# Lending the idle two-bank tile to the scans in an attention and Fourier-mixing kernel

## The chip, the cores and the metric

The kernel runs on one core of one Trainium2 chip. The metric is the device time of one execution in microseconds. Three runs of the kernel before gave a median of 1719.29 us (1718.14 to 1720.03).

Six names stand for the parts of a core. TensorE (PE in the profile) multiplies matrices and writes into PSUM, a small memory of eight banks; a bank holds 512 float32 values for each of 128 partitions. Its weight loads have a row of their own (PEld). VectorE (DVE) and ScalarE (ACT) work element by element and can read PSUM. GpSimd (POOL) works on SBUF alone. SyncE (SP) issues transfers. Each engine takes its instructions strictly in the order in which the program lists them, and waits on semaphores where one needs another's result or a buffer that another still uses.

## What is computed

The input `x` is 2048 tokens of 512 numbers. Two mixings of it are weighed by a gate per token:

```
g = sigmoid(sum(x * gate_w))
a = softmax attention of x, 32 heads of 16, 2048 x 2048 scores each, then @ wo
b = real part of the Fourier transform along the 512 and along the 2048
    a' = x @ dft_hid_re.T ; b' = x @ dft_hid_im.T
    y  = dft_seq_re @ a' - dft_seq_im @ b'
out = g * a + (1 - g) * b
```

The weights `wqkv` and `wo` are scaled up by 64, so the scores are large and the softmax needs the maximum of every row of scores before it can take exponentials.

## The kernel before

The kernel works in two stages. The front (to about 649 us) computes queries, keys and values, then the Fourier part's first product along the 512, then the larger part of its second product along the 2048. The second stage runs attention proper, with the rest of the Fourier part and the output projection between its steps.

To keep float32 accuracy every operand of a product is split into a high and a low part, and each product is three matmuls. `halves_of` (line 199) issues each of these as two matmuls, on the upper and the lower 64 rows of the array, which run side by side and write two PSUM banks; the two banks are added later. Here "product pair" means such two matmuls. They are all recorded under line 203.

**Scans.** The row maxima are found ahead of the attention. A scan covers 128 queries and 512 keys for the two heads of a pair; there are 64 for each of 16 pairs. 740 of them run in the front, woven between the product pairs. A scan in the front (`scan_folded`, line 159) has two halves, j = 0 and j = 1, one per head. A half is one matmul into one bank (line 172). Then, for every even block of keys, ScalarE copies the bank with a ReLU into an SBUF tile `fold` (line 176); for every odd block VectorE adds the bank to `fold` and takes the maximum along the row (line 178). The keys had been prepared as differences, so that sum and ReLU together give the maximum of both blocks.

**Slots and pace.** `products` and the loop of the spectral part call `beside` after each product pair. That is a slot. `beside` counts it, runs what `after` has put off to this slot, and issues a scan whenever the pace says so: one in 2.03 slots (`PART`) through most of the spectral part, one in 2.85 (`SWAP`) where operands are exchanged. When scan n comes, its half j = 0 is issued, and right behind it the half j = 1 of scan n - 1 (`behind`), so that the two matmuls fall on different rows of the array and run side by side.

**PSUM.** Four banks are two wide tiles of two banks, `wide0` and `wide1`; the products of one output tile accumulate in one of them and the next output tile takes the other (`xy`). The other four banks are the beds of the scans, `d0`, `d1`, `k0`, `k1`: an even block of keys goes to d, an odd one to k, the number is j. So a half of a scan finds its bank free when the same half two scans before has been read.

**The spectral part.** From about 326 us on, an output tile t is 48 slots: 16 steps of three product pairs. Its coefficients are loaded on SyncE's queue and split by GpSimd. At the end of a tile ScalarE reads its first bank at once (`tx`) and the second five slots later (`ty`), both scaled by `gm`; GpSimd adds them. The other wide tile meanwhile takes the next t. So for most of the 48 slots one wide tile holds no data that is needed. Tiles 14 and 15, and later 0 and 1 of the second half (`ph` = 1), are computed two at a time and use both wide tiles.

**What sets the order.** The order on each engine is written out by the program: the loops, `after` and the pace. A framework adds the semaphore waits. It takes them from tiles: whoever writes into a tile waits for those who have read it, and a new tile in the place of an old one (same tag) waits for the uses of the old. The pools here release whole tiles (`reuse_waits="tile"`).

Of the kernel before, what the change touches and what calls it, by code (L numbers as in the profile page):

```python
# [24 lines left out]
NB = S // P  # L25
# [40 lines left out]
def build(tc, xT, wqkv, wo, wrT, wiT, cr, ci, ct, gate, out):  # L66
    nc = tc.nc
    with ExitStack() as ctx:
# [90 lines left out]
        def scan_folded(n, j, bank, pool):  # L159

            p, i = SEQ[n]
            qb, c = i // 4, i % 4
            if i == 0 and j == 0:
                new_maxima(p)
                if p in PARTS:
                    nc.vector.memset(mx[p], -3.0e38)
            qs, ks = scanned[p]  # L170
            b, ps = 64 * j, bank(f"{'dk'[c % 2]}{j}")
            nc.tensor.matmul(ps, qs[b:b + 48, qb * P:(qb + 1) * P], ks[b:b + 48, c * 512:(c + 1) * 512],  # L172
                             start=True, stop=True)
            if c % 2 == 0:
                fold[j] = pool.tile([P, 512], F32, tag=f"fold{j}", name="fold")
                nc.scalar.activation(fold[j], ps, AF.Relu)  # L176
            else:
                nc.vector.tensor_tensor_reduce(out=fold[j], in0=ps, in1=fold[j], scale=1.0, scalar=-3.0e38,  # L178
                                               op0=ALU.add, op1=ALU.max, accum_out=mx[p][:, j, qb, c // 2:c // 2 + 1])
# [28 lines left out]
        turns = [0]  # L208

        def wide(i, name):  # L210
            return psf.tile([P, 2, 512], F32, tag=f"wide{i}", name=name)
# [21 lines left out]
        def narrow(tag, name):  # L233
            return psk[0].tile([P, 512], F32, tag=tag, name=name)

        def bank():

            order_.append(order_.pop(0))
            return narrow(order_[-1], "s2")
# [27 lines left out]
        seen, slots, due, count = [0], [0], [], [0]  # L267
        pace = [None, 0.0]
        with ExitStack() as pf:
# [3 lines left out]

            pss1 = []

            def xy():
                turns[0] += 1
                ps = wide(turns[0] % 2, "xy")
                return ps[:, 0, :], ps[:, 1, :]

            def after(n, f, *args):

                count[0] += 1
                due.append((slots[0] + n, count[0], f, args))
# [3 lines left out]
            def run_due(force=(False, False)):  # L288

                while True:  # L290
                    ready = [d for d in due if d[0] <= slots[0] or force[d[2] in maxima]]
                    if not ready:
                        return
                    d = min(ready, key=lambda d: d[:2])
                    due.remove(d)
                    d[2](*d[3])  # L296
# [88 lines left out]
            def begin_folds():  # L385

                banks.close()
                psk.append(ctx.enter_context(tc.tile_pool(name="psk", bufs=1, space=PSUM, reuse_waits="tile")))
                beds.extend((lambda tag: narrow(tag, "s"), fp))

            with ExitStack() as px:
                wb = px.enter_context(tc.tile_pool(name="wb", bufs=1))
# [235 lines left out]
            with ExitStack() as py:  # L628
                cp = py.enter_context(tc.tile_pool(name="cp", bufs=2, reuse_waits="tile"))
                def fetch(n):  # L630
                    if n < len(coef):
                        load_coef(n, cp.tile([P, CS, P], F32, tag="craw", name="craw", bufs=7))

                for n in range(4, 10):
                    fetch(n)
                for d in range(4):
                    after(4 + 6 * d, split_operand, NB - 4 + d, tail[:, d, :], nc.gpsimd)
                scan_at(SWAP)
                after(24, scan_at, PART)
                pss, yre, early = {}, {}, {}  # L640

                def go_ahead(k):

                    if k == 0:
                        assert seen[0] == FRONT, (seen, pace)
                        scanned.update(unfolded)
                        sums.append(narrow("k1", "pvb"))
                        nc.vector.memset(sums[0], 0.0)
                    if k == 1:
                        e = next_eb()  # L650
                        ahead.append(qk_single(0, 0, 0, [e[:, j, :] for j in range(2)]))
                    elif k == 2:
                        scan(seen[0], wide(1 - SCANS_IN, "s1"))
                        seen[0] += 1
                    else:
                        ahead.append(qk_both(0, 0, k // 3))

                def mixed(ph, t, yre, tx, ty):
                    y = cp.tile([P, D], F32, tag="y", name="y")
                    nc.gpsimd.tensor_add(y, tx, ty)  # L660
                    if ph:
                        nc.gpsimd.tensor_add(y, y, yre)
                    after(14, nc.sync.dma_start, y_d[t // 4][:, t % 4, :], y)

                for n, (ph, t, u) in enumerate(coef):
                    prepare(n + 3)
                    fetch(n + 10)
                    if u == 0 and (ph, t) == (0, NB - 1):
                        scan_at(SWAP)
                    if u == 2 and (ph, t) == (1, 0):  # L670
                        scan_at(PART)
                    if n == len(coef) - 2 * NU:
                        for _ in load_use(0):
                            pass
                        unfolded[PART_PAIR], loads = row_loads(PART_PAIR, nc.sync)
                        for load in loads:
                            load()
                    hi, lo = ready.pop(n)
                    if u == 0:
                        pss[t] = xy()  # L680
                        if ph:
                            yre[t] = cp.tile([P, D], F32, tag="yre", name="yre")
                            nc.sync.dma_start(yre[t], y_d[t // 4][:, t % 4, :])
                    if (ph, t, u) == (0, NB - 3, 0):
                        for i in range(2):
                            raw = stk.tile([P, 4, D], F32, tag="stk", name="early")
                            for d in range(4):
                                early[4 * i + d] = raw[:, d, :]
                                after(24 * i + 6 * d, nc.sync.dma_start, raw[:, d, :], ab_d[1][4 * i + d])
                    swap = (ph, t) == (0, NB - 1)  # L690

                    def renew(s):
                        raw = early.pop(s)
                        ah[s], al[s] = block(2 * s), block(2 * s + 1)
                        nc.scalar.copy(ah[s], raw)
                        after(4, (nc.gpsimd if s % 4 == 3 else nc.vector).tensor_sub, al[s], raw, ah[s].bitcast(F32))
                        if s >= 8 and s + 5 < NB:
                            early[s + 5] = load_operand(1, s + 5, cp)

                    for w in range(CS):  # L700
                        s = u * CS + w
                        for i, (c_, a_) in enumerate(((hi, ah[s]), (hi, al[s]), (lo, ah[s]))):
                            halves_of(pss[t], c_[:, w, :], a_, s == 0 and i == 0, s == NB - 1 and i == 2)
                            beside()
                            if n >= len(coef) - NU and 3 * s + i in AHEAD:
                                go_ahead(AHEAD.index(3 * s + i))
                        if swap:
                            if 3 <= s < 8:
                                early[s + 5] = load_operand(1, s + 5, cp)
                            after(1 + 5 * (s % 8) + 4 * (s // 8), renew, s)  # L710
                    if u == NU - 1:
                        tx = cp.tile([P, D], F32, tag="tx", name="tx")
                        last = n == len(coef) - 1
                        ty = cp.tile([P, D], F32, tag="raw" if last else "ty", name="ty", bufs=5 if last else 2)
                        if last:
                            for v, ps in zip((tx, ty), pss[t]):
                                nc.vector.tensor_scalar_mul(v, ps, gm[:, t:t + 1])
                        else:
                            nc.scalar.mul(tx, pss[t][0], gm[:, t:t + 1])
                            after(5, nc.scalar.mul, ty, pss[t][1], gm[:, t:t + 1])  # L720
                        after(10, mixed, ph, t, yre.get(t), tx, ty)
                run_due((True, True))

        assert seen[0] == FRONT + 1 and turns[0] % 2 == SCANS_IN, (seen, turns)
# [580 lines left out]
```

## Time and profile before

| | |
|---|---|
| median of 3 runs | 1719.29 us |
| profiled execution, time | 1718.53 us |
| its span | 1716.7 us |
| TensorE busy | 1702.1 us |
| ScalarE busy | 1535.5 us |
| VectorE busy | 1158.0 us |
| GpSimd busy | 726.6 us |
| scans in the front: matmuls, 1480 | 58.8 to 649.0 us |
| granted TensorE clock | 0.999 |

How to read it: the span is the profiled execution from its first instruction to its last, and its time has 1.8 us around that. A row of a timeline gives start, duration, engine, line, operation, what is written and read, and how many instructions are merged; in brackets stands the idle time before and what ended it. A row of the table of waits reads "who waits, its line <- whom, its line: us in total, times, longest". A row of the table by stretches gives, for each engine, its busy time and in brackets its instructions. "Busy" of TensorE counts matmuls that overlap and whose ends are modelled, so a busy TensorE can still be waiting a little.

### The profile page before, as it was taken

The numbers are of one execution on the slowest core, as the hardware profiler recorded it, in microseconds if no ns is written. First come the engines' busy times: TensorE is split into PE (matmuls) and PEld (weight loads), VectorE is DVE, ScalarE is ACT, GpSimd is POOL, SyncE is SP. The second block draws the span as 40 slices with busy tenths as digits, with TensorE's granted clock in tenths as the row PEclk, the third lists the DMA queues.
The fourth block names the chain that finished last, engine by engine and source line by source line (L and its number), as shares of the span: only waits on it lengthen the run. The fifth ranks groups of instructions, "written<-read, shape, count | busy, mean of one in ns | idle before, by whom it ended". The sixth has DMA issues, their size and how long they took to land.

```text
span 1716.7 us, 36848 instructions
## 1 busy us (share of the span) xinstructions
PE 1702.1 (99%) x13560; PEld 1027.3 (60%) x13560; DVE 1158.0 (67%) x2310; ACT 1535.5 (89%) x2548; POOL 726.6 (42%) x875
## 2 busy tenths in 40 slices
PE   9999999999999999999999999999999999999998
PEld 6888888888989784333333333334555555555554
DVE  5788988899999996666666666666212456653343
ACT  5798889888888888999999999999888888888876
POOL 4352233855555761444455364444223333334222
PEclk9999999999999999999999999999999999999999
DMA  8783444634344774455445354453426465575833
GB/s 284 243 299 74 130 145 160 202 113 118 113 118 137 197 147 100 120 126 123 133 119 136 93 142 123 114 153 73 91 63 144 134 148 148 142 174 151 197 88 126
DMA packets 149573, 242.04 MB, mean 141 GB/s; under 512 B 50144, under 2 KB 60880, under 8 KB 142800
## 3 DMA queue, kind: packets, MB, share of 16 engines
q1 hardware_dynamic: 134128, 218.32, 46.6%
q0 software_dynamic: 14688, 20.33, 5.0%
q8 instruction: 106, 1.74, 0.5%
q10 hardware_dynamic: 576, 1.05, 0.2%
q14 instruction: 75, 0.61, 0.1%
HBM read 156.24 MB, written 83.11 MB: 139 GB/s over the span
## 4 chain that ended last, share of the span: by engine, by line
PE 94%; DMA 2%; DVE 1%; issue 1%; ACT 1%; POOL 1%; SPq 0%; DVEq 0%; POOLq 0%; ACTq 0%
PE pvb L751 28%; PE xy L203 23%; PE s L228 18%; PE s L172 11%; PE s L203 9%; PE s L153 4%; DVE fold L178 1%; DMA raws<-wqkv 0%; ACT fold L176 0%; DMA q_d<-eh 0%; DMA raws<-xT 0%; PE s L548 0%; DVE y L866 0%; POOL s L296 0%; DMA k_d<-eh 0%
## 5 line engine op out<-in xcount | busy, mean ns | idle before, releaser
L252 ACT ACTIVATE eb<-s 128x1024 f32<-128x1024 f32 x512 | 576.6, 1126 | 66.4 <-PE s L228 66.4
L260 ACT ACTIVATE e<-s 128x512 f32<-128x512 f32 x1022 | 606.9, 705 | 0.0
L178 DVE CUSTOM_DVE_ANT_0 fold<-s,fold 128x512 f32<-128x512 f32 x740 | 496.7, 690 | 53.7 <-PE s L172 17.2
L751 PE MATMUL pvb<-eb,va 128*17 128x512 f32 x2052 | 511.5, 597 | 0.0
L751 PE MATMUL pvb<-e,va 128*17 128x512 f32 x2044 | 510.7, 597 | 0.0
L176 ACT ACTIVATE fold<-s 128x512 f32<-128x512 f32 x740 | 435.2, 603 | 72.7 <-PE s L172 46.9
L155 DVE TENSOR_REDUCE mx<-s 128x2 f32<-128x1024 f32 x284 | 348.0, 1225 | 173.6 <-PE s L153 173.5
L228 PEld LDWEIGHTS s<-qs,ks 50*128 50x128 f32 x2048 | 214.7, 184 | 349.3 <-ACT eb L252 242.2
L228 PE MATMUL s<-qs,ks 50*128 50x512 f32 x2048 | 417.3, 434 | 0.0
L203 PE MATMUL xy<-b,c 64*128 64x512 f32 x2304 | 377.7, 392 | 1.2 <-DVE b L347 1.0
L172 PE MATMUL s<-ks,qs 48*128 48x512 f32 x1480 | 366.3, 406 | 2.1 <-DVE mx L178 0.7
L203 PEld LDWEIGHTS xy<-b,c 64*128 64x128 f32 x2304 | 264.4, 187 | 17.3 <-DVE b L347 1.4
L172 PEld LDWEIGHTS s<-ks,qs 48*128 48x128 f32 x1480 | 199.8, 184 | 57.7 <-DVE mx L178 17.8
L751 PEld LDWEIGHTS pvb<-eb,va 128*17 128x17 f32 x2052 | 71.3, 96 | 191.5 <-issue 183.0
L203 PE MATMUL s<-b,b 64*128 64x512 f32 x1050 | 136.8, 391 | 0.1
L770 POOL DMA_DIRECT2D r_d<-lc x31 | 18.0, 580 | 262.3 <-DVE lc L769 215.1
L203 PE MATMUL xy<-w,b 64*128 64x512 f32 x768 | 123.3, 392 | 0.0
L763 POOL DMA_DIRECT2D lc<-ob x124 | 63.0, 515 | 130.8 <-DVE ob L760 120.5
L153 PE MATMUL s<-ks,qs 48*128 48x512 f32 x568 | 114.7, 394 | 0.0
L203 PEld LDWEIGHTS s<-b,b 64*128 64x128 f32 x1050 | 100.3, 185 | 24.0 <-issue 1.0
L378 POOL TENSOR_TENSOR c<-craw,c 128x512 fp32r<-128x512 f32 x76 | 99.8, 1313 | 6.1
L772 POOL DMA_DIRECT2D rb<-r_d x124 | 60.4, 494 | 96.3 <-DMA r_d<-lc 91.3
(143 smaller groups left out, 1587.9 us busy)
## 6 DMA issues: line engine op xcount, KB each, us to landing
qs<-q_d SPq DMA_DIRECT2D x68, 256.0 KB
craw<-cr SPq DMA_DIRECT2D x60, 256.0 KB
craw<-ct SPq DMA_DIRECT2D x48, 256.0 KB
ks<-k_d SPq DMA_DIRECT2D x42, 256.0 KB
kept_None<-sum SPq DMA_DIRECT2D x40, 256.0 KB
craw<-kept_None SPq DMA_DIRECT2D x40, 256.0 KB
qs<-q_d SPq DMA_DIRECT2D x68, 128.0 KB
craw<-ci SPq DMA_DIRECT2D x32, 256.0 KB
```

The costliest lines, as they stand in the source:

```text
L153: nc.tensor.matmul(ps[:, j, :], qs[b:b + 48, qb * P:(qb + 1) * P], ks[b:b + 48, c * 512:(c + 1) * 512], start=True, stop=True)
L155: nc.vector.tensor_reduce(mx[p][:, :, qb, c], ps, axis=AX.X, op=ALU.max)
L172: nc.tensor.matmul(ps, qs[b:b + 48, qb * P:(qb + 1) * P], ks[b:b + 48, c * 512:(c + 1) * 512], start=True, stop=True)
L176: nc.scalar.activation(fold[j], ps, AF.Relu)
L178: nc.vector.tensor_tensor_reduce(out=fold[j], in0=ps, in1=fold[j], scale=1.0, scalar=-3.0e38, op0=ALU.add, op1=ALU.max, accum_out=mx[p][:, ...
L203: nc.tensor.matmul(ps[j], lhs[r], rhs[r], start=first, stop=last)
L228: nc.tensor.matmul(pss[j], ks[b:b + 50, kb * P:(kb + 1) * P], qs[b:b + 50, q0:q0 + 512], start=True, stop=True)
L252: nc.scalar.activation(e, ps, AF.Exp, scale=SCALE)
L260: nc.scalar.activation(e[j], pss[j], AF.Exp, scale=SCALE)
L378: sub(lo, raw, hi.bitcast(F32))
L751: nc.tensor.matmul(pvb[r:r + VC, :], va[:, kb, 2 * p + j, :], es[c][j], start=kb == 0, stop=kb == NB - 1, tile_position=(0, r))
L763: nc.gpsimd.dma_start(lc[32 * n:32 * n + 32, :], ob[r + DH:r + VC, :].rearrange("p (s e) -> p s e", e=16))
```

## The change

`bank(...)` of the scans is no longer chosen by the parity of the key block but by a function `bed`. The two wide tiles are allocated once, as `sides`, for the whole front, and `xy` hands out their banks by turns. At the end of an output tile t, with 0 < t < 13, `spare` notes which side that tile has used and a stretch of slots, from 12 to 44 after the current one. While the slot count lies in it, `bed` has three places for a scan: d, k and the spare side ("w"); it takes the one that was dealt longest ago. Outside it there are d and k. A scan keeps its place for both halves: bank j of the side, or the bed with number j. Pace, scans, readers and all other code stay.

```diff
@@ scan_folded
-            b, ps = 64 * j, bank(f"{'dk'[c % 2]}{j}")
+            b, ps = 64 * j, bank(n, j)
@@
+            sides = [wide(i, "xy") for i in range(2)]
+            spare = [0, 0, 0]
+            places, taken = {"d": -2, "k": -1}, {}
+
             def xy():
                 turns[0] += 1
-                ps = wide(turns[0] % 2, "xy")
+                ps = sides[turns[0] % 2]
                 return ps[:, 0, :], ps[:, 1, :]
+
+            def bed(n, j):
+
+                if j == 0:
+                    side, since, until = spare
+                    free = ["d", "k"] + ["w"] * (since <= slots[0] < until)
+                    at = min(free, key=lambda a: places.get(a, -3))
+                    places[at] = n
+                    taken[n] = at, side
+                at, side = taken[n]
+                return sides[side][:, j, :] if at == "w" else narrow(f"{at}{j}", "s")
@@ begin_folds
-                beds.extend((lambda tag: narrow(tag, "s"), fp))
+                beds.extend((bed, fp))
@@ the spectral part
-                pss, yre, early = {}, {}, {}
+                pss, yre, early, side_of = {}, {}, {}, {}
@@
                         pss[t] = xy()
+                        side_of[t] = turns[0] % 2
@@ at the end of tile t
                         after(10, mixed, ph, t, yre.get(t), tx, ty)
+                        if 0 < t < NB - 3:
+                            spare[:] = side_of[t], slots[0] + 12, slots[0] + 44
```

## The prediction

> **What bounds the kernel now.** I read the page first (engines, slices, chain), then the stretches of the spectral part one by one, then the order of single instructions there.
>
> ```profile
> span 1716.7 us, 36848 instructions
> PE 1702.1 (99%) x13560; PEld 1027.3 (60%) x13560; DVE 1158.0 (67%) x2310; ACT 1535.5 (89%) x2548; POOL 726.6 (42%) x875
> PE 94%; DMA 2%; DVE 1%; issue 1%; ACT 1%; POOL 1%; SPq 0%; DVEq 0%; POOLq 0%; ACTq 0%
> PE pvb L751 28%; PE xy L203 23%; PE s L228 18%; PE s L172 11%; PE s L203 9%; PE s L153 4%; DVE fold L178 1%; DMA raws<-wqkv 0%; ACT fold L176 0%; DMA q_d<-eh 0%; DMA raws<-xT 0%; PE s L548 0%; DVE y L866 0%; POOL s L296 0%; DMA k_d<-eh 0%
> ```
>
> TensorE ends nearly everything: 94% of the chain. So a microsecond that TensorE loses in its own queue is lost to the kernel, and a saving elsewhere counts only if TensorE was waiting for it. In the spectral part (about 326 to 649 us) the queue holds product pairs (L203) with scans (L172) between them.
>
> ```profile
> core 0: us, PE busy (x) PEld busy (x) DVE busy (x) ACT busy (x) POOL busy (x), PEclk, DMA share, GB/s
> 490.00:520.00 30.00, 30.00 (x256) 25.47 (x254) 28.46 (x85) 26.32 (x46) 15.96 (x17) 1.00 0.47 132
> 580.00:610.00 30.00, 29.67 (x243) 24.23 (x241) 28.36 (x75) 25.39 (x47) 21.61 (x19) 1.00 0.84 199
> ```
>
> An undisturbed stretch issues 256 matmuls in 30 us, 0.234 us per concurrent pair; the granted clock is 1.00. What waits there for a bank is this:
>
> ```profile
> engine line waited for: us in total, times, longest us
> PEld s L172 <- DVE mx L178: 8.7, 35, 0.7
> PEld s L172 <- ACT fold L176: 4.7, 16, 0.3
> PEld s L172 <- DVE mx L178: 0.5, 2, 0.3
> ```
>
> The first two rows are the whole spectral part, 326 to 650 us; the third is 407 to 418 us, the part of one tile in which the change lends its idle neighbour. Asked over all 14 such parts, seven show this row at all, with 0.2 to 0.5 each and 2.4 us together. So the waits that a third place for the scans can remove are about 2.4 us, 0.14% of the time. VectorE is 95% busy in the undisturbed row, but it does not hold TensorE up there.
>
> **The rhythm of the scans.** TensorE, ScalarE and VectorE over two and a half microseconds of that part:
>
> ```profile
> 485.46 0.45 PE L172 MATMUL s<-ks,qs 48*128 48x512 f32 x2
> 485.70 0.69 PE L203 MATMUL xy<-b,c 64*128 64x512 f32 x4
> 486.17 0.46 PE L172 MATMUL s<-ks,qs 48*128 48x512 f32 x2
> 486.40 0.69 PE L203 MATMUL xy<-b,c 64*128 64x512 f32 x4
> 486.87 0.46 PE L172 MATMUL s<-ks,qs 48*128 48x512 f32 x2
> ...
> 485.95 1.24 ACT L176 ACTIVATE fold<-s 128x512 f32<-128x512 f32 x2 [0.16 <-PE s L172]
> ...
> 486.01 0.69 DVE L178 CUSTOM_DVE_ANT_0 fold<-s,fold 128x512 f32<-128x512 f32 x1
> ...
> L172 PE MATMUL s<-ks,qs x1480: 386/397/502, 58.8 to 649.0; 48*128 48x512 f32 x185
> ```
>
> Each L172 row of two is the first half of one scan and, 0.06 to 0.07 us later (0.46 less one matmul of 0.397), the second half of the scan before. The rows are 0.70 us apart, so a second half starts 0.77 us after its own first half. The reading of a first half ends later than that: the first half at 485.46 is read by VectorE at 486.01 for 0.69, to 486.70, 1.24 us after it started; the one at 486.17 is read by the second of the two ScalarE instructions, which end at 487.19, 1.02 us after.
>
> **The change, part by part.**
>
> *Order of work.* Instruction for instruction, all five engines and the DMA queues keep their order: 740 scans at the same pace, the same 1480 matmuls, 740 reads. Only banks, and so waits, change. Nothing is moved past anything, so cost 0: there is no instruction or transfer that would need new cover.
>
> *One tile object per side instead of a new one per product.* Within `products` nothing changes; ten waits of TensorE on its own earlier matmuls go. Cost 0: the matmul waited for is long done in TensorE's own queue; were each a release of 0.07 us (below), it would be 0.7 us gained.
>
> *The lent place.* From 12 to 44 slots after a product ends, `bed` deals three places in turn, so every third scan goes to the wide tile: 78 scans in 14 stretches, 38 read by ScalarE and 40 by VectorE. Its two halves are two banks of one tile object. Beds `d` and `k` are two tiles of one bank each. The program as built draws the consequence: in all 78 lent scans the matmul of the second half carries a wait for the instruction that reads the first half, although that lies in the other bank. In the kernel before, a second half waits only for the reading of the scan two before it. So the wait comes 0.77 us after the first half starts, and what it waits for ends at 1.02 or 1.24. Behind it on TensorE's queue stands everything: the product pairs and the next scan; nothing passes it.
>
> The trace has one clean wait of this kind, of another cause, which prices the restart:
>
> ```profile
> 415.27 0.44 PE L172 MATMUL s<-ks,qs 48*128 48x512 f32 x2
> 415.97 0.78 PE L172 MATMUL s<-ks,qs 48*128 48x512 f32 x2
> 416.87 0.59 PE L172 MATMUL s<-ks,qs 48*128 48x512 f32 x2
> 417.67 0.48 PE L172 MATMUL s<-ks,qs 48*128 48x512 f32 x2
> ...
> 416.26 0.18 PEld L172 LDWEIGHTS s<-ks,qs 48*128 48x128 f32 x1 [0.33 <-DVE mx L178]
> ...
> 415.50 0.69 DVE L178 CUSTOM_DVE_ANT_0 fold<-s,fold 128x512 f32<-128x512 f32 x1 [0.39 <-PE xy L203]
> ```
>
> VectorE ends at 416.19 and the weight load goes at 416.26: 0.07 from release to start. The second matmul of the row at 415.97 was due at about 416.02 and so came 0.24 late. The next two rows stand 1.70 us after it instead of 1.40, so 0.24 of waiting cost 0.30: restarting, with its weights not loaded ahead, takes 0.06 more. By the third row the pair is 0.48 wide again, so each third scan meets the old rhythm.
>
> Per lent scan: read by ScalarE, 1.02 + 0.07 - 0.77 + 0.06 = 0.38 us; read by VectorE, 1.24 + 0.07 - 0.77 + 0.06 = 0.60 us. Sum 38 x 0.38 + 40 x 0.60 = 14.4 + 24.0 = 38.4 us. Four of the 78 have a third slot between the halves (0.235 less each) and the last has none (about 0.5 more): -0.5. The bounds: each wait as the one above, 78 x 0.30 = 23.4 us; each as long as the longest in the table of waits, 78 x 0.7 = 54.6 us. I take the middle sum since it is built from the very instructions that will be waited for.
>
> *The tile's return.* The next product on that side starts at slot 48, the last lent scan before slot 44 with its second half two or three slots later. Ten of the 14 starts now wait for a lent scan's read. A read ends up to 1.24 us after its matmul, three slots are about 1.1 us (0.70 for two, with a scan): late by 0.1 to 0.2 plus a restart where it is late at all. Bounds 0 and 14 x 0.5; I take 5 x 0.28 = +1.4 us.
>
> *Waits relieved.* Scans in `d` and `k` beside a lent one find their bank free a scan sooner. At most 2.4 us (above); part of it is lost anyway because the engines read as before. I take -1.0.
>
> ```profile
> L176 ACTq EVENT_SEMAPHORE  x710: 17/17/17, 63.3 to 648.2; - x178
> ```
>
> *ScalarE's extra waits.* 173 of these 710 go, 17 ns each, 2.9 us of ScalarE's queue. ScalarE has room in the rows above (26.32 of 30 us), so 0; were it the bound, this would be the gain.
>
> Sum: 38.4 - 0.5 + 1.4 - 1.0 = +38.3 us on the profiled execution's 1718.53 us (span 1716.7 and 1.8 around it; 0.8 below the median of the runs, 1719.29): 1757 us.
>
> A rule that would promise the contrary: the Trainium skill's "Perfetto Trace Analysis", section "Optimizing Tensor Performance", says that independent matmul groups should rotate through different PSUM banks, so that the reading of one overlaps the matmuls of the next. By it alone the sum would be the 2.4 us above as a gain, 1716 us. The trace agrees that little is waited for there, and the rule does not speak of two banks that are waited for as one.
>
> **The rivals.**
>
> *The wait does not bite.* If the two halves were free of each other on the chip as banks are, only the relief is left: 1718.5 - 2.4 = 1716 us, no change that a measurement shows (it tells about 0.2%, 3.4 us). It decides if the first half's reading ends under 0.70 us after its matmul's start; both rows above end at 1.02 and 1.24, and the shortest ScalarE part of that is a matmul of 0.397 and a read of 0.60. Beside it, the skill's "PSUM — Partial Sum Buffer", section "PSUM bank collisions raise a hardware error", asks that accesses be guarded by bank and quadrant, so the chip would not need this wait; the program has it all the same. Chance 0.05, and 0.02 for more gain than 3.4 us.
>
> *The halves stay apart.* If after a wait the second halves kept lagging (the row at 416.87 is 0.59 wide, 0.13 more than usual) until the next lent scan, each wait would find 0.13 us already spent: 78 x 0.13 = 10.1 us less, 1747 us. The row at 417.67 speaks against it. Chance 0.13.
>
> *The clock falls.* Many small waits could cost TensorE its clock over the 148 us of lent stretches; at half the clock a second half would come after 1.54 us, past both reads, so the waits would vanish and 148 us be added: 1867 us. Against it: 580 to 610 us has several waits and keeps 1.00.
>
> ```profile
> PEld s L172 <- DVE mx L178: 2.5, 7, 0.7
> ```
>
> That row is 578 to 602 us, with 7 waits in 24 us; the change puts six in 11 us, of 0.3 to 0.5. The skill's "TensorE: Matmul & The Clock Gate", section "A second HAM failure mode: psum-queue depth-cycling", describes a clock that drops in such cycling. Chance 0.02.
>
> **How the numbers follow.** The forecast has 0.78: 1757 us. The range takes in the halves staying apart, a restart that costs nothing (78 x 0.06 = 4.7 less), and above it reads that find their engine busy (0.1 us more on each: 7.8): 1738 to 1768 us. Slower holds 0.78 + 0.13 + 0.02 = 0.93, within 0.2% 0.05, faster 0.02.
>
> **What would show it.** In the changed kernel's profile: the row of TensorE's weight load at the scans' line waiting for VectorE and ScalarE grows from 13.4 us in 51 waits to over 35 us, with 78 more; the spectral part is some 38 us longer and all before and after it is not; in a lent stretch every third scan is followed by a gap, wider after a VectorE read; idle of ScalarE and VectorE grows there. Wrong would be: no such row (the wait does not bite), a gap of under 0.2 us (the halves stay apart), or a granted clock under 1.00.

## The result, and the profile after

The changed kernel takes 1758.1 us (median of 4 runs, 1757.54 to 1759.81); the kernel before took 1719.66 us beside it. The ratio is 1.0224, 95% interval 1.0206 to 1.0241: 38.4 us slower. The forecast was 1757 us, 1738 to 1768. The profiled execution took 1758.19 us, its span is 39.7 us longer than before.

The page of the changed kernel, the rows that answer to those shown of before:

```profile
span 1756.4 us, 36685 instructions
PE 1730.1 (99%) x13560; PEld 1015.6 (58%) x13560; DVE 1159.0 (66%) x2310; ACT 1530.9 (87%) x2548; POOL 727.3 (41%) x875
PE 93%; DVE 3%; DMA 1%; issue 1%; ACT 1%; POOL 0%; SPq 0%; DVEq 0%; ACTq 0%; POOLq 0%
PE pvb L769 28%; PE xy L203 21%; PE s L228 18%; PE s L203 10%; PE s L172 9%; PE s L153 4%; PE xy L172 3%; DVE fold L178 2%; ACT fold L176 1%; DMA raws<-wqkv 0%; DMA q_d<-eh 0%; DVE mx L178 0%; DMA raws<-xT 0%; PE s L563 0%; DVE y L884 0%
```

The engines do the same amount of work. In the chain VectorE's share has gone from 1% to 3%: there TensorE stands still until VectorE has read. Where it stands is told by the same row of the second stage in both kernels, the first matmuls of attention proper (before, then after; the columns after the count are shortest, median and longest ns, then first and last start):

```profile
L751 PE MATMUL pvb<-eb,va x2052: 592/592/606, 656.2 to 1700.9; 128*17 128x512 f32 x187
```

```profile
L769 PE MATMUL pvb<-eb,va x2052: 592/592/606, 697.1 to 1741.2; 128*17 128x512 f32 x187
```

The second stage starts 40.9 us later and ends 40.3 us later. So nothing happened in it; the front has the loss. Nearly all of that is the spectral part's: ScalarE's reading `tx` starts 1.1 us later than before at the end of the first output tile (334.4 us before, 335.5 after) and 39.2 us later at the last (640.6, 679.8). The scans, the stretch 490 to 520 us and the waits of the spectral part in the changed kernel:

```profile
L172 PE MATMUL s<-ks,qs x1324: 386/397/500, 59.9 to 688.8; 48*128 48x512 f32 x190
L172 PE MATMUL xy<-ks,qs x156: 386/493/501, 356.1 to 690.0; 48*128 48x512 f32 x156
```

```profile
490.00:520.00 30.00, 29.00 (x219) 20.96 (x217) 24.12 (x73) 22.48 (x42) 14.18 (x15) 1.00 0.26 81
```

```profile
PEld xy L172 <- DVE mx L178: 34.7, 72, 1.2
PEld xy L172 <- ACT fold L176: 15.8, 38, 0.4
PEld s L172 <- DVE mx L178: 6.0, 25, 0.8
PEld s L172 <- ACT fold L176: 3.9, 13, 0.3
PEld xy L203 <- issue: 2.4, 6, 0.5
```

The 156 matmuls of the 78 lent scans are the row `xy<-ks,qs`. In 30 us 219 matmuls are issued where 256 were, at the same granted clock of 1.00. The weight loads of the ordinary scans (`s`) wait a little less than before: 9.9 us, once 13.4. Those of the lent scans (`xy`) wait 50.5 us, in 110 waits: 38 for ScalarE, and 72 for VectorE. That is more than the 38.4 us lost, since the table counts how long the row of weight loads is idle; in the place below it is idle for 0.76 us and the row of matmuls for 0.32.

The last row has no counterpart before. These six are the first weight loads of a product that takes back a lent side. The table puts them down to `issue`, a wait for nothing that the profile shows, but each follows the reading of the last lent scan's second half by 0.11 to 0.12 us. Behind VectorE's reading (four of them) the product starts 0.21 to 0.22 us late, behind ScalarE's (two) not at all: 0.9 us together.

Here is one place with a lent scan and the next lent one (two ordinary scans lie between them): TensorE's matmuls and weight loads, then VectorE.

```profile
379.07 0.40 PE L172 MATMUL xy<-ks,qs 48*128 48x512 f32 x1
380.50 0.50 PE L172 MATMUL xy<-ks,qs 48*128 48x512 f32 x1 [0.32 <-DVE mx L178]
381.89 0.50 PE L172 MATMUL xy<-ks,qs 48*128 48x512 f32 x1
383.07 0.50 PE L172 MATMUL xy<-ks,qs 48*128 48x512 f32 x1
```

```profile
380.49 0.18 PEld L172 LDWEIGHTS xy<-ks,qs 48*128 48x128 f32 x1 [0.76 <-DVE mx L178]
381.89 0.18 PEld L172 LDWEIGHTS xy<-ks,qs 48*128 48x128 f32 x1 [0.17 <-DVE mx L178]
383.07 0.18 PEld L172 LDWEIGHTS xy<-ks,qs 48*128 48x128 f32 x1 [0.43 <-ACT fold L176]
```

```profile
379.75 0.69 DVE L178 CUSTOM_DVE_ANT_0 fold<-xy,fold 128x512 f32<-128x512 f32 x1
381.14 0.69 DVE L178 CUSTOM_DVE_ANT_0 fold<-xy,fold 128x512 f32<-128x512 f32 x1 [0.70 <-PE xy L172]
```

The first half of a scan starts at 379.07. VectorE reads it from 379.75 to 380.44, and at 380.50 the second half goes, 1.43 us after the first where it had been 0.77. VectorE, idle for 0.70 us, reads that from 381.14 to 381.83. The first half of the next lent scan then starts at 381.89: it too has waited, for the reading of the other bank of the same tile. Its own second half waits for ScalarE, to 383.07, 1.18 us after. Followed scan by scan through the trace, all 78 second halves start right behind the reading of their first half: 0.052 us behind ScalarE's (median of 38, the longest 0.125) and 0.063 us behind VectorE's (40). And 32 first halves, all of scans that ScalarE reads, start 0.060 to 0.064 us behind VectorE's reading of the second half of the lent scan before.

### The profile page after: what moved, and what is told of

Same layout as the page of the kernel before. It is cut to its first block, busy times and chain, and to the rows that moved or that the text cites. A ratio compares the mean times of both kernels' runs of the same rounds, so it can differ in the third digit from the quotient of the medians.

```text
span 1756.4 us, 36685 instructions
## 1 busy us (share of the span) xinstructions
PE 1730.1 (99%) x13560; PEld 1015.6 (58%) x13560; DVE 1159.0 (66%) x2310; ACT 1530.9 (87%) x2548; POOL 727.3 (41%) x875
## 3 DMA queue, kind: packets, MB, share of 16 engines
q10 hardware_dynamic: 576, 1.05, 0.2%
## 4 chain that ended last, share of the span: by engine, by line
PE 93%; DVE 3%; DMA 1%; issue 1%; ACT 1%; POOL 0%; SPq 0%; DVEq 0%; ACTq 0%; POOLq 0%
PE pvb L769 28%; PE xy L203 21%; PE s L228 18%; PE s L203 10%; PE s L172 9%; PE s L153 4%; PE xy L172 3%; DVE fold L178 2%; ACT fold L176 1%; DMA raws<-wqkv 0%; DMA q_d<-eh 0%; DVE mx L178 0%; DMA raws<-xT 0%; PE s L563 0%; DVE y L884 0%
## 5 line engine op out<-in xcount | busy, mean ns | idle before, releaser
L178 DVE CUSTOM_DVE_ANT_0 fold<-s,fold 128x512 f32<-128x512 f32 x660 | 446.5, 689 | 66.5 <-ACT fold L176 29.7
L176 ACT ACTIVATE fold<-s 128x512 f32<-128x512 f32 x664 | 388.7, 604 | 91.7 <-PE s L172 74.1
L203 PE MATMUL xy<-b,c 64*128 64x512 f32 x2304 | 398.6, 396 | 1.7 <-DVE b L362 1.2
L203 PEld LDWEIGHTS xy<-b,c 64*128 64x128 f32 x2304 | 269.5, 186 | 33.6 <-issue 2.4
L172 PEld LDWEIGHTS s<-ks,qs 48*128 48x128 f32 x1324 | 193.3, 184 | 45.1 <-DVE mx L178 15.0
L392 POOL CAST c<-craw 128x512 fp32r<-128x512 f32 x76 | 47.6, 627 | 152.1 <-PE xy L203 113.5
```

Source lines behind the costliest of these rows:

```text
L203: nc.tensor.matmul(ps[j], lhs[r], rhs[r], start=first, stop=last)
```

## The experiments

Theory: the loss is the wait between two halves that lie in two banks of one tile object. Rivals: lending itself costs (the tile comes back late, readers get mixed); the objects that live through the front cost; the price belongs to a stretch and not to a scan. Each ratio is to the kernel before on the same chip, with its 95% interval.

**Two tile objects.** Each half of a side gets an object of its own. Nothing else changes: the same 78 scans, places, readers and order.

```diff
-            sides = [wide(i, "xy") for i in range(2)]
+            sides = [[psx[i].tile([P, 512], F32, tag=f"x{i}{j}", name=f"xy{i}{j}") for j in range(2)] for i in range(2)]
...
-                return sides[side][:, j, :] if at == "w" else narrow(f"{at}{j}", "s")
+                return sides[side][j] if at == "w" else narrow(f"{at}{j}", "s")
```

(The two pools `psx` are closed where attention first takes a wide tile, and the wide tiles follow in their place.)

> The changed kernel, but each half of a lent scan lies in a tile object of its own (one bank each); 78 scans are lent as before, and no second half waits for the reading of its own first half. Theory of the wait (the cost is that wait): 38 to 40 us go, 1717 to 1720 us, and no row of the scans' weight loads with 78 waits more. Rival (lending itself costs: the tile comes back late to the next product, or readers are mixed badly over the places): still 1750 to 1760 us.

1718.3 us, ratio 0.9993 (0.9985 to 1.0002). The whole loss is gone, with the lending still there. The table of waits of its spectral part has no row of a lent scan's weight load; the waits for banks are these:

```profile
PEld s L175 <- DVE mx L181: 6.0, 25, 0.7
PEld s L175 <- ACT fold L179: 4.6, 14, 0.7
PEld xy L206 <- DVE mx L181: 1.3, 4, 0.4
```

10.6 us for the scans where it was 13.4, and 1.3 us new at the products (L206), where the tile comes back. So the third place relieves the scans a little, and in the time nothing of it can be measured.

**Nothing lent.** The objects and `bed` stay, but "w" is never free.

```diff
-                    free = ["d", "k"] + ["w"] * (since <= slots[0] < until)
+                    free = ["d", "k"] + ["w"] * (since <= slots[0] < since)
```

> The changed kernel with its two tile objects allocated once and its function that deals the places, but nothing is ever lent. Theory of the wait: 1719 to 1720 us, the same as before. Rival (the tile objects that live through the whole front cost something of their own): over 1725 us.

1719.04 us, ratio 0.9999 (0.9990 to 1.0008). The objects that live long cost nothing that can be measured.

**The second half first, in one object.** A lent scan's second half is issued before the reading of its first half stands in the program.

```diff
-                    scan_folded(n, 0, *beds)
-                    done = behind(n - 1)
+                    scan_folded(n, 0, *beds, "write")
+                    if taken[n][0] == "w":
+                        done = behind(n - 1)
+                        scan_folded(n, 1, *beds, "write")
+                        scan_folded(n, 0, *beds, "read")
+                        scan_folded(n, 1, *beds, "read")
+                    else:
+                        scan_folded(n, 0, *beds, "read")
+                        done = behind(n - 1)
...
```

(Left out here: `scan_folded` is split into its write and its read, and `behind` passes over lent scans.)

> The changed kernel with one tile object per side as there, but the second half of a lent scan is issued before the reading of its first half stands in the program, right behind the second half of the scan before. So the second half has no wait for the reader; places, readers, stretches and the 78 lent scans stay. Theory of the wait: 1717 to 1721 us. Rival (the tile object or the bank itself is slow, whatever the order of issue): 1750 to 1760 us.

1724.8 us, ratio 1.0027 (1.0017 to 1.0038): 5.2 us slower, so a seventh of the loss stays, more than I had expected. The table of waits has one row of lent scans:

```profile
PEld xy L175 <- DVE mx L184: 9.1, 30, 0.3
```

Second halves wait for their own reader no more; 30 lent scans still wait for VectorE. Scan by scan, these are first halves: 30 of them, all of scans that ScalarE reads, start 0.061 to 0.070 us behind VectorE's reading of the second half of the lent scan before, the other wait of the one object. Thirteen of the 14 stretches (each from three scans ahead of its first lent one to three behind its last; the fourteenth ends with the front) take 191.0 us in the kernel before, 228.9 in the changed one and 195.9 here. Some of the 4.9 us may come from the six returns to a product that wait here too, and from the new order of the matmuls; that was not separated.

**One reader at a time.** Only scans read by ScalarE, or only those read by VectorE, may be lent. Both give 54 lent scans, four apart. The edit for ScalarE is shown; for VectorE the last number is 1.

```diff
-                    free = ["d", "k"] + ["w"] * (since <= slots[0] < until)
+                    free = ["d", "k"] + ["w"] * (since <= slots[0] < until and SEQ[n][1] % 2 == 0)
```

> Only scans that ScalarE reads may be lent: 54 scans in the same 14 stretches. Theory of the wait: 54 x 0.38 = 20.5 us over the kernel before by the terms of the prediction (21.6 with the 0.40 us measured in the changed kernel), 1740 to 1742 us. Rival (a cost per stretch, 38.4 / 14 = 2.7 us, whatever is lent in it): 1758 us.

> Only scans that VectorE reads may be lent: 54 scans in the same 14 stretches. Theory of the wait: 54 x 0.60 = 32.4 us over the kernel before by the terms of the prediction (34.6 with the 0.64 us measured in the changed kernel), 1752 to 1755 us. Rival (a cost per stretch): 1758 us; rival (a price per lent scan that does not depend on the reader, 0.49 us): 1746 us for this and for the one with ScalarE alike.

ScalarE alone: 1733.9 us, ratio 1.0083 (1.0067 to 1.0098), 14.1 us or 0.26 us per lent scan. VectorE alone: 1749.1 us, ratio 1.0178 (1.0164 to 1.0192), 29.3 us or 0.54 us per lent scan. By the intervals either price can be off by some 0.05 us. The two rows of lent weight loads, of the one and of the other:

```profile
PEld xy L172 <- ACT fold L176: 22.9, 53, 0.5
```

```profile
PEld xy L172 <- DVE mx L178: 40.4, 54, 1.1
```

The price goes by scan and by reader, so the rivals of a cost per stretch and of one price for all fall. But ScalarE's is well under the 0.38 us forecast. The trace says why: in these runs each second half follows the first half of the next scan by 0.23 us (median) where it was 0.06 us before, from one lent scan to the next. The two streams of matmuls, first halves on the upper rows of the array and second halves on the lower, stay apart after a wait. So a second half comes 0.94 us after its first without any wait, and only the rest is waited for. For ScalarE's scans the reading ends 1.05 us after the first half starts, close to the 1.02 forecast, so the wait shrinks. For VectorE's it ends at 1.37 instead of 1.24 (medians), and little of the gain is left.

**Five apart, mixed readers; six apart, VectorE alone.** The runs with one reader leave 38.4 - 38 x 0.26 - 40 x 0.54 = 6.9 us of the changed kernel unexplained, give or take some 4 us by the intervals of the three runs. Two more runs asked where it belongs.

```diff
-                    free = ["d", "k"] + ["w"] * (since <= slots[0] < until)
+                    free = ["d", "k"] + ["w"] * (since <= slots[0] < until and n - places.get("w", -9) >= 5)
```

> The changed kernel, but a scan is lent only five or more scans after the last lent one: 51 lent scans (25 read by ScalarE, 26 by VectorE), none of whose first halves waits for the last lent scan's second half. Theory that the price is 0.26 and 0.54 us per wait of a second half, as the two runs with one reader gave, and that the rest of the changed kernel's 38 us is another wait, that of the first half for the second half of the lent scan three before: 25 x 0.26 + 26 x 0.54 = 20.5 us, 1740 us. Rival (every lent scan costs the 0.49 us that the changed kernel shows on average): 51 x 0.49 = 25 us, 1745 us.

1743.8 us, ratio 1.0140 (1.0126 to 1.0154): 24.2 us for 51 lent scans, 21.7 to 26.5 by the interval. The rival (25 us) lies in it and my theory (20.5 us) does not, though its two prices bring an uncertainty of about 2 us of their own. So mixing probably costs more than the two prices even where no first half waits for the lent scan before.

For the next run the condition is `SEQ[n][1] % 2 == 1` and six apart.

> Only scans that VectorE reads are lent, and each six scans after the last: 41 lent scans. With four between (the run with VectorE's readers alone) no bed that VectorE frees is wanted again two scans later; here one is, right behind each lent scan. Theory (a wait of a lent second half makes VectorE's reads late, and the next place that such a late read frees makes TensorE wait a second time, 0.1 to 0.2 us): 41 x 0.54 + 41 x 0.15 = 28 us, 1746 to 1750 us, and first halves in an ordinary bed that start 0.06 us after VectorE's read of the scan two before. Rival (0.54 us per lent scan, whatever else lies around it): 22 us, 1741 to 1742 us.

1743.2 us, ratio 1.0129 (1.0115 to 1.0143), 22 us for 41 lent scans: 0.54 each, the rival's number. The wait that the theory named is there: the first half four scans behind a lent one starts 0.061 to 0.064 us behind VectorE's reading of the scan two before it, in 36 of the 41 places, and the next first half follows it after 0.80 us on average instead of 0.71. But it adds nothing to the total. It closes the lag between the streams, and the interval in which the next lent second half waits is shorter for it: 1.21 us, 1.28 in the run with VectorE alone and four apart. So the theory of a second price fell too.

Most of what is left can be placed. In the changed kernel the three intervals around a lent scan of ScalarE's (from the first half of the scan before to that of the second after) last 2.56 us on average, and 2.42 with ScalarE alone. That is 0.14 x 38 = 5.4 of the 6.9 us. For VectorE's the sums are 2.70 and 2.72. The extra lies on both sides of the lent scan's first half (0.81 and 0.79 us, with ScalarE alone 0.72 and 0.72), not in the interval in which its second half waits (0.95 and 0.97). That first half waits for VectorE, and the streams close up from 0.23 to 0.11 us.

Five apart the same sum is 2.48 us, and there another wait closes the streams to 0.11 us: behind 21 of the 26 lent scans that VectorE reads, the first half four scans on, just ahead of the next lent one, starts 0.062 to 0.066 us behind VectorE's reading of its ordinary bed. So both kinds of wait stand where the extra is. How much of it is the waiting of the 32 first halves and how much the closing up was not separated.

**The same wait without any lending.** The kernel before, with `d0` and `d1` as the two banks of one object.

```diff
-            b, ps = 64 * j, bank(f"{'dk'[c % 2]}{j}")
+            b, ps = 64 * j, bank('dk'[c % 2], j)
...
+                d_bed = d_bed.tile([P, 2, 512], F32, tag="dd", name="dd")
+                beds.extend((lambda bed, j: d_bed[:, j, :] if bed == "d" else narrow(f"k{j}", "s"), fp))
```

> The kernel before, nothing lent, but the beds d0 and d1 are the two banks of one tile object for the whole front. Theory of the wait: every even scan's second half waits for ScalarE's reading of its first, and its first half for the reading of the second half two scans before, so two scans take at least twice 1.09 us where 1.41 us were needed in the spectral part and about 1.75 in the part before: some 217 x 0.77 + 152 x 0.43, less in the exchange of operands, 200 to 230 us more, 1920 to 1950 us. Rival (the cost belongs to the lending alone): 1719 us.

2006.7 us, ratio 1.1667 (1.1649 to 1.1684), 287 us slower. The direction and the cause are the expected ones, the size is beyond the expected 230:

```profile
PEld dd L172 <- ACT fold L176: 348.8, 738, 1.2
```

```profile
L172 PE MATMUL dd<-ks,qs x740: 392/496/500, 59.2 to 937.5; 48*128 48x512 f32 x185
```

738 of the 740 matmuls into that object wait for ScalarE. From half to half it is 1.183 us (median), where I had put 1.09: a matmul that has waited lasts 0.496 us instead of 0.397, since its weights are loaded only then, and the reading that the next half waits for begins that much later. Two scans take 2.367 us (median) in the projections and the spectral part alike, against a median of 1.66 before in the projections and 1.41 in the spectral part.

**Two objects, lent longer.** From 8 to 47 slots, and after tile 0 too: 104 scans.

```diff
-                        if 0 < t < NB - 3:
-                            spare[:] = side_of[t], slots[0] + 12, slots[0] + 44
+                        if t < NB - 3:
+                            spare[:] = side_of[t], slots[0] + 8, slots[0] + 47
```

> One tile object per half, as in the run that does so, and lent from 8 to 47 slots instead of 12 to 44 and after tile 0 too: 104 scans instead of 78. Theory (there is little to win since TensorE waits for banks only some 2.4 us in all these stretches): 1717 to 1719 us, within 0.2% of the kernel before. Rival (the third place wins in proportion to its use): 0.5 to 1 us less than the run with 78, not to be told from it. A late return of the tile to the next product would show as over 1720 us.

1726.1 us, ratio 1.0028 (1.0017 to 1.0039): 4.9 us slower. It is the late return that the expectation had only as a sign of being wrong.

```profile
PEld xy L206 <- DVE mx L181: 4.3, 8, 0.6
PEld xy L206 <- ACT fold L179: 4.0, 7, 0.7
PEld xy L206 <- issue: 3.1, 7, 0.6
```

These are 22 waits of the products, 11.4 us, where the shorter stretch has 1.3. All of them, those put down to `issue` too, start 0.05 to 0.13 us behind the reading of a lent scan. So of the four slots that the shorter stretch leaves free at its end, more than one was needed. The earlier start and tile 0 were not tried alone.

## Why the prediction was right

*The bound.* TensorE's queue ends nearly everything, and what it lost it lost for good: the second stage moved by 40.9 us as a block, and 38 us of that came in the spectral part, as forecast.

*The wait.* Right in every point named: 78 second halves, each right behind the reading of its first, with everything behind them in the queue. Two objects take the loss away, the second half issued first takes six sevenths of it, and the same wait without lending makes its own loss.

*The price.* The sum was 38.4 us for the waits and 38.3 in all; measured are 38.4 by the medians. That it is so close is luck: the terms were not so good, and their errors cancel. Forecast were 0.38 us per scan that ScalarE reads and 0.60 per one that VectorE reads; alone they cost 0.26 and 0.54, together 31.5 us. What was wrong in it is the reading of one event, "by the third row the pair is 0.48 wide again, so each third scan meets the old rhythm". The rival of the halves that stay apart was right in the runs with one reader: 0.23 us instead of 0.06, from one lent scan to the next. In the changed kernel they stay 0.23 us apart up to VectorE's lent scans and close to 0.11 ahead of ScalarE's, at a price.

*What was not priced.* That a first half waits for the other bank as well: 32 of them, which the forecast did not name. They stand in the 72 waits for VectorE where 40 were expected. They lie where 5.4 of the other 6.9 us are.

*The tile's return.* +1.4 us forecast, from waits at ten of the 14 starts. The changed kernel has six waits of this kind, and four of them make a product late, by 0.9 us together: the mechanism is right and the size a little high. Two objects with the same stretch have four waits, 1.3 us of idle weight loads; the longer stretch has 11.4.

*Waits relieved.* -1.0 us forecast, from 2.4 that were there. With two objects the median was 1.5 us better, with an interval from 2.6 us better to 0.3 us worse. The forecast lies in it; the runs can't say more.

*The zeros.* The long-lived objects cost nothing that can be measured (nothing lent: ratio 0.9999). ScalarE's event waits fell by 173 as forecast, from 710 to 537; a gain from it can't be told apart in the time, and ScalarE is idle more than before (busy 87% of the span, once 89%).

*The other rivals.* The wait bites, so that one falls. The clock stayed at 1.00 all through the spectral part (in every row of 30 us); 110 waits of 0.15 to 1.23 us did not bring it down. The rule of the Trainium skill on rotating through PSUM banks ("Perfetto Trace Analysis", "Optimizing Tensor Performance") has its trial in the run with two objects: one place more in the rotation does no harm there and gains nothing measurable, as few waits on banks were left to remove (2.4 us in these stretches).

## What to carry to other kernels

In this program a matmul waits for those who use its tile object, not only its bank: two banks in one object cost 38.4 us here, the same banks in two objects nothing. Before two halves with different readers share a tile, look at which instruction each write waits for in the built program, and give each bank an object of its own where one half is written after the other is read. A third buffer can save no more than about the waits for buffers that the trace shows in just those stretches (2.4 us here), and a lent buffer has to be back some slots before its owner needs it: lent three slots longer, and begun earlier, it cost 4.9 us.

## What was not expected of the hardware

A matmul whose weight load had to wait lasts 0.496 us instead of 0.397 in the trace. The end of a matmul is modelled, but ScalarE's reading bears it out: in the changed kernel it starts 0.53 us after a lent first half that has waited and 0.44 us after one that has not. In a loop of write, read and write again this is paid each time: 1.183 us from half to half (one object for d0 and d1), where the sum of the rows of an undisturbed stretch gave 1.09.

TensorE's two streams of matmuls, on the upper and the lower rows, stayed 0.23 us apart from one lent scan to the next, where they were 0.06 us apart before. A second half that would have to wait then starts later by itself. Waits in one queue therefore don't simply add up: ScalarE's cost 0.26 us each among their like, and more where something between them closed the streams up again.
